# A second network's first layer as seven half products instead of eight (Strassen's scheme, one level), in a fused attention and two-network kernel

## The chip, the core and the metric

The kernel runs on one core of a Trainium2 chip. The metric is device time in microseconds (us) of one execution; the median of 3 runs of the kernel before is 708.27 us (708.18 to 709.79). About 0.3% is what a comparison of this kernel can tell from no change. Engines: PE is TensorE (matmuls; PEld its weight loads), DVE is VectorE, ACT is ScalarE, POOL is GpSimd, SP starts the transfers (DMA).

## What is computed

The reference, cut to what matters here. An attention with random features gives x with 1152 tokens and 512 columns; two networks follow:

```python
def _moe_ref(x, w_in, w_out):            # x 1152 x 512, inner width 2048
    h = x @ w_in
    return (h - np.tanh(h)) @ w_out

def _moe2_ref(x, domain_probs, w1, w2):  # E = 4 experts, inner width F = 1024
    p = domain_probs / (domain_probs.sum(-1, keepdims=True) + 1e-09)
    out = np.zeros((N, D))
    for e in range(E):
        h = np.maximum(x @ w1[e], 0.0)
        out += p[:, e:e + 1] * (h @ w2[e])
    return out
```

The change is in `x @ w1[e]` of the second network.

## The kernel before

Every float32 operand of a product is held as a high and a low part (`split`, L70 and L71: ACT writes the high part, DVE or POOL the rest), and a product is three matmuls: high by high, high by low, low by high. Sums run in PSUM, which has 8 banks of 512 float32 columns.

The kernel has three stages. Attention lies first; while it ends, `early` computes the first network's first layer for its first unit, in the PSUM tiles `ps_e` (2 banks). The pools of attention are opened in the order `ps_e`, `ps_t`, `ps_p`, `ps_n`, two banks each, and closed together. The first network then runs in 4 units of 512 inner columns: `hidden` (L433) computes 128 inner columns for all 1152 tokens in three blocks of 384, `minus_tanh` the activation (L443 to L452, with L450 as the last reader of the PSUM tile), `out_a` (L536) the second layer. Its orders on PE, DVE and ACT are written by hand (`tc.manual_schedule`).

The second network runs in 8 units of 512 inner columns, two for each expert, of 4 steps with 128 each. A step is `hidden` (36 matmuls of 384 columns: 4 parts of the contraction, 3 splits, 3 token blocks), `activated` (ACT L463 writes the high part of the ReLU, DVE L464 the low part), and a quarter of the previous unit's output: `out_b(i, t)` for token tile t is 12 matmuls of 512 columns into a tile of `ps_o` (2 banks, L558), and DVE adds that, times the expert's share, to `oacc` (L562; L560 in the first unit). The order is the planner's: a list of instructions by priority of program order, with buffers that make one wait for another. The weights come by DMA (four of 256 KB for two steps) into `rawp` (4 buffers) and are split by ACT and DVE.

Where things lie: the activations g of a unit are in pool `hpa` for even units and in `hpb` for odd ones; the second layer's weights in `wp` for even and in `wp2` for odd units. After attention the PSUM pools are opened in the order `ps_hb` (3 banks), `ps_ha` (3 banks), `ps_o` (2 banks). The `x` operands of the second network are `x2` (named y in the trace).

Of the kernel before, what the change touches and what calls it, by code (L numbers as in the profile page):

```python
# [18 lines left out]
T2 = 0.01  # L19
# [7 lines left out]
def tile_favor_attention__then__two_moe(  # L27
# [18 lines left out]
    nc = tc.nc  # L46
    B, H, S, D = q.shape
    M = omega.shape[0]
    N, DM = out.shape
# [8 lines left out]
    NJ = UF // P  # L58
    CH = 384
    NC = N // CH  # L60
    scale = 1.0 / float(D) ** 0.25
    assert B == 2 and 2 * D == P and M == P and S == TB * P + P // 2 and NT == 2 * TB + 1

# [5 lines left out]
    def split(hi, lo, src, eng_lo=None):  # L69
        nc.scalar.activation(hi, src, AF.Copy)  # L70
        (eng_lo or nc.vector).tensor_tensor(out=lo, in0=src, in1=hi.bitcast(F32), op=ALU.subtract)  # L71

    def run(todo):
        for step in todo:
            step()

    def interleave(*streams):

        todo = []
        for i, s in enumerate(streams):  # L80
# [4 lines left out]
    units = [("a", u) for u in range(DFF // UF)] + [("b", e, f) for e in range(E) for f in range(F // UF)]  # L85
    NA = DFF // UF
    steps = [(i, j) for i in range(len(units)) for j in range(NJ)]
    wa, wb, late = {}, {}, {}

    class Decoded:  # L90
# [14 lines left out]
        def topped(self):  # L105


            m = self.m = decp.tile([P, UF], I32, tag="m", name="m", bufs=3)
            nc.scalar.activation(m, self.low.bitcast(U32), AF.Copy, scale=2.0**-29 * (1 - 2.0**-18), bias=-0.49999)  # L109

        def joined(self):
            if self.m is None:
                m = self.m = decp.tile([P, UF], I32, tag="m", name="m", bufs=3)
# [31 lines left out]

    def load_a(i, j):

        f0 = units[i][-1] * UF + j * P
        if units[i][0] == "a":
            return Decoded(w_in[:, f0:f0 + P].rearrange("(c p) n -> p c n", p=P), "wa")  # L150
        return Loaded(w1[units[i][1], :, f0:f0 + P].rearrange("(c p) n -> p c n", p=P), "wa", wp)

    def load_b(i, j):

        f0 = units[i][-1] * UF
        if units[i][0] == "a":
            return Decoded(w_out[f0:f0 + UF, j * P:(j + 1) * P].rearrange("(c p) n -> p c n", p=P), "wb")
        rows = w2[units[i][1], f0 + j * P:f0 + (j + 1) * P, :]
        return Loaded(rows.rearrange("p (c n) -> p c n", c=1), "wb", late["wp"] if i % 2 else wp)
# [295 lines left out]
    def activated(i, j, eng_lo=None):  # L455
        new_g(i, j)
        hh, hl = gs[i, j]
        ps = ph[i, j][:, :, :CH]
        if units[i][0] == "a":
# [84 lines left out]
    def out_b(i, t):  # L544

        e = units[i][1]
        if i == NA and t == 0:
            state["acc"] = accp.tile([P, NT, DM], F32, tag="acc", name="oacc")
        s = slice(t * P, (t + 1) * P)
        last = (i, t) == (len(units) - 1, NT - 1)  # L550
        for c in (slice(0, DM // 2), slice(DM // 2, DM)) if last else (slice(0, DM),):
            acc = state["acc"][:, t, c]
            full = ps_o.tile([P, 512], F32, tag="o", name="po")
            po = full[:, :c.stop - c.start]
            for j in range(NJ):
                (wh, wl), (gh, gl) = wb[i, j], gs[i, j]
                for z, (w, g) in enumerate(((wh, gh), (wl, gh), (wh, gl))):
                    nc.tensor.matmul(po, g[:, s], w[:, c], start=j == 0 and z == 0, stop=j == NJ - 1 and z == 2)  # L558
            if i == NA:
# [5 lines left out]
            if i == len(units) - 1:  # L565
                for b in range(B):
                    for t0, t1, r0, r1, ss in token_rows(b):
                        if t0 <= t < t1:
                            rows = out[b * S + ss.start:b * S + ss.stop, c].rearrange("(r t) c -> r t c", t=t1 - t0)
                            nc.sync.dma_start(out=rows[:, t - t0, :], in_=acc[r0:r1, :])  # L570

    def out_steps(i, j):
        return [lambda t=t: out_b(i, t) for t in range(j * NT // NJ, (j + 1) * NT // NJ)]

# [23 lines left out]
    with tc.manual_schedule(engines={mybir.EngineType.DVE, mybir.EngineType.PE, mybir.EngineType.Activation}):  # L598
# [40 lines left out]
    for s in range(END, END + 3):  # L639
        ready(load_a, wa, *steps[s])  # L640
    moe1.close()
    late["wp"] = ctx.enter_context(tc.tile_pool(name="wp2", bufs=NJ, side="right", reuse_waits="tile"))
# [10 lines left out]
    for n in range(1, NC):  # L653
        for j in range(2):
            hidden(NA, j, [n])
    for s in range(NA * NJ, len(steps) + NJ):
        i, j = steps[s] if s < len(steps) else (len(units), s - len(steps))
        g = []
        if s < len(steps):
            if s - NA * NJ > 1:  # L660
                hidden(i, j)
            g = activated(i, j)
            ready(load_b, wb, i, j)
            if s + 3 < len(steps):
                ready(load_a, wa, *steps[s + 3])
        interleave(g, out_steps(i - 1, j) if i > NA else [])


# [28 lines left out]
```

## Time and profile before

| | before |
|---|---|
| median of 3 runs | 708.27 us (708.18 to 709.79) |
| the profiled execution, its own time | 710.09 us |
| its span, first to last instruction | 708.2 us |
| PE busy | 691.7 us (98%) |
| DVE busy | 387.3 us (55%) |
| ACT busy | 287.8 us (41%) |
| mean granted clock of PE | 0.998 |

Attention ends at about 110 us, the first network at about 310, and the second takes the rest. Matmuls overlap, so the busy time of PE counts stretches in which at least one runs; the price of one in a dense stream is the distance from its start to the next one's.

### The profile page before, as it was taken

How to read it: one execution, taken by the hardware profiler on the slowest of the kernel's cores; microseconds unless marked ns; L12 is line 12 of the kernel's file. 1: busy time of each engine (PE TensorE's matmuls, PEld its weight loads, DVE VectorE, ACT ScalarE, POOL GpSimd, SP SyncE). 2: the span in 40 equal slices, each digit the busy share in tenths (PEclk: the TensorE clock that was granted, in tenths of full speed). 3: DMA queues.
4: the chain of work that ended last, by engine and by line, in shares of the span. 5: the costliest groups of instructions: out<-in, count | busy, mean ns of one | idle time of the engine just before them, and what ended most of it. 6: DMA issues, size and time to landing. Idle time of an engine off the chain costs nothing.

```text
span 708.2 us, 9667 instructions
## 1 busy us (share of the span) xinstructions
PE 691.7 (98%) x3897; PEld 643.8 (91%) x3897; DVE 387.3 (55%) x562; ACT 287.8 (41%) x517; POOL 60.3 (9%) x58
## 2 busy tenths in 40 slices
PE   6999998999999999999999999999999999999998
PEld 6999897999999999899898998989989899998986
DVE  4699888699999887554325234234332333243132
ACT  5799897777576674243113012112122121030100
POOL 1032024322221210000000000000000000000000
PEclk9999999999999999999999999999999999999999
DMA  8952100122122110032103012012102111000012
GB/s 218 288 169 90 62 31 5 57 86 94 60 90 90 59 61 31 1 89 90 31 16 88 17 30 75 16 31 75 31 24 66 30 60 46 15 16 1 0 45 89
DMA packets 50412, 43.69 MB, mean 62 GB/s; under 512 B 6080, under 2 KB 45248, under 8 KB 50368
## 3 DMA queue, kind: packets, MB, share of 16 engines
q1 hardware_dynamic: 50368, 43.09, 20.2%
q8 instruction: 30, 0.49, 0.3%
q14 instruction: 14, 0.11, 0.1%
HBM read 40.72 MB, written 2.36 MB: 61 GB/s over the span
## 4 chain that ended last, share of the span: by engine, by line
PE 78%; DVE 11%; ACT 6%; issue 2%; DMA 2%; SPq 1%; POOL 0%; DVEq 0%
PE psh L433 32%; PE po L558 28%; PE po L536 7%; PE pse L433 3%; PE psP L292 3%; PE psN L344 2%; DVE y L450 2%; DVE y L447 2%; DVE y L448 1%; ACT y L444 1%; DVE psh L449 1%; DVE m L119 1%; ACT u L443 1%; DVE m L118 1%; ACT m L109 1%
## 5 line engine op out<-in xcount | busy, mean ns | idle before, releaser
L433 PE MATMUL psh<-y,wah 128*128 128x384 f32 x768 | 157.2, 336 | 0.1
L433 PEld LDWEIGHTS psh<-y,wah 128*128 128x128 f32 x768 | 135.7, 188 | 3.5 <-issue 0.4
L558 PE MATMUL po<-wbl,hh 128*128 128x512 f32 (+1 forms) x292 | 114.4, 392 | 0.0
L558 PE MATMUL po<-wbh,hh 128*128 128x512 f32 (+1 forms) x292 | 113.9, 390 | 0.0
L558 PE MATMUL po<-wbh,hl 128*128 128x512 f32 (+1 forms) x292 | 113.3, 389 | 0.0
L70 ACT ACTIVATE wah<-raw 128x512 fp32r<-128x512 f32 x32 | 20.2, 633 | 201.6 <-PE psh L433 201.6
L433 PE MATMUL psh<-y,wal 128*128 128x384 f32 x384 | 89.9, 336 | 0.0
L562 DVE SCALAR_TENSOR_TENSOR oacc<-po,pr,oacc 128x512 f32<-128x512 f32 (+1 forms) x64 | 47.5, 742 | 74.1 <-PE po L558 74.1
L71 DVE TENSOR_TENSOR wal<-raw,wah 128x512 fp32r<-128x512 f32 x32 | 22.1, 691 | 118.4 <-ACT wah L70 118.3
L433 PEld LDWEIGHTS psh<-y,wal 128*128 128x128 f32 x384 | 68.6, 188 | 0.0
L558 PEld LDWEIGHTS po<-wbh,hl 128*128 128x128 f32 x292 | 54.9, 188 | 12.2
L558 PEld LDWEIGHTS po<-wbh,hh 128*128 128x128 f32 x292 | 54.8, 188 | 11.4
L558 PEld LDWEIGHTS po<-wbl,hh 128*128 128x128 f32 x292 | 54.9, 188 | 10.7
L464 DVE SCALAR_TENSOR_TENSOR hl<-psh,hh 128x1152 fp32r<-128x1152 f32 x32 | 43.4, 1357 | 34.5 <-ACT hh L463 34.4
L536 PE MATMUL po<-hh,wbh 128*128 128x384 f32 x180 | 60.9, 339 | 0.2
L536 PE MATMUL po<-hl,wbh 128*128 128x384 f32 x180 | 60.8, 338 | 0.2
L536 PE MATMUL po<-hh,wbl 128*128 128x384 f32 x180 | 60.6, 336 | 0.5 <-POOL wbl L71 0.5
L433 PE MATMUL psh<-x,wah 128*128 128x384 f32 x288 | 57.9, 336 | 0.6 <-ACT wah L70 0.6
L433 PEld LDWEIGHTS psh<-x,wah 128*128 128x128 f32 x288 | 50.5, 188 | 0.8 <-ACT wah L70 0.8
L463 ACT ACTIVATE hh<-psh 128x1152 fp32r<-128x1152 f32 x32 | 35.8, 1120 | 37.7 <-PE psh L433 37.7
L70 ACT ACTIVATE wbh<-raw 128x512 fp32r<-128x512 f32 x32 | 20.3, 633 | 63.4 <-PE po L558 30.6
L451 ACT ACTIVATE hh<-y 128x1152 fp32r<-128x1152 f32 (+3 forms) x24 | 20.4, 848 | 42.9 <-DVE y L450 42.9
(102 smaller groups left out, 1050.1 us busy)
## 6 DMA issues: line engine op xcount, KB each, us to landing
raw<-in_moe_w_dram SPq DMA_DIRECT2D x64, 256.0 KB, 2.7
raw<-in_moe_w_in_dram SPq DMA_DIRECT2D x16, 512.0 KB, 3.7
raw<-in_moe_w_out_dram SPq DMA_DIRECT2D x16, 512.0 KB, 3.4
kn<-in_k_dram SPq DMA_DIRECT2D x8, 256.0 KB, 4.1
vs<-in_v_dram SPq DMA_DIRECT2D x8, 256.0 KB, 4.6
qn<-in_q_dram SPq DMA_DIRECT2D x8, 256.0 KB, 4.9
out_dram<-oacc SPq DMA_DIRECT2D x7, 256.0 KB, 2.3
out_dram<-oacc SPq DMA_DIRECT2D x4, 128.0 KB, 2.1
```

The lines of the kernel that those rows point to most:

```text
L70: nc.scalar.activation(hi, src, AF.Copy)
L71: (eng_lo or nc.vector).tensor_tensor(out=lo, in0=src, in1=hi.bitcast(F32), op=ALU.subtract)
L292: nc.tensor.matmul(ps[:, i].rearrange("p a m -> p (a m)"), x[:, c], o, start=j == 0, stop=j == 2)
L344: nc.tensor.matmul(ps[:, j, h, :ZC], qt[g][:, j, h, :], kvz[p][:, t // (TB + 1), h, :], start=True, stop=True)
L433: nc.tensor.matmul(ph[i, j][:, n, :CH] if bank is None else bank, w[:, c], x[:, n * CH:(n + 1) * CH] if bank is None else x[:, n], start=z ...
L447: a=lambda: vec.scalar_tensor_tensor(out=y, in0=y, scalar=CB, in1=u, op0=ALU.add, op1=ALU.mult),
L451: h=lambda: act.activation(hh, y, AF.Copy),
L463: lambda: nc.scalar.activation(grid(hh), ps, AF.Relu),
L464: lambda: nc.vector.scalar_tensor_tensor(out=grid(hl), in0=ps, scalar=0.0, in1=grid(hh).bitcast(F32), op0=ALU.max, op1=ALU.subtract),
L536: nc.tensor.matmul(po[:, :CH], w[:, r], g[:, s], start=j == 0 and z == 0, stop=j == NJ - 1 and z == 2,)
L558: nc.tensor.matmul(po, g[:, s], w[:, c], start=j == 0 and z == 0, stop=j == NJ - 1 and z == 2)
L562: nc.vector.scalar_tensor_tensor(out=acc, in0=po, scalar=pr[:, t, e:e + 1], in1=acc, op0=ALU.mult, op1=ALU.add)
```

## The change

The second network's inner columns are cut into 16 pairs (`pairs`) of 2 x 128. For the last 14 of them (`PLAIN = 2` pairs stay as they were) the product of a pair's weights (a 2 x 2 matrix of blocks: 2 halves of inner columns, 2 halves of the contraction) with x (2 halves of the contraction, 2 halves of 576 tokens) is made by Strassen's scheme in Winograd's form: seven products of blocks in place of eight, each 2 contraction parts x 3 splits x 2 column blocks of 288. Sums of x (`token_sums`, T1 to T4) are made once, by DVE, and split; sums of weights (`Sums.added`, S1 to S4) are made by DVE for each pair and split, one pair ahead. Three PSUM tiles of two banks (`ps_y`: Y1, Y2, Y3) take the products, some accumulate on what stands there, and DVE adds across them (`add`). ACT then writes the high and DVE the low part of the ReLU, quarter by quarter.

A unit is now a pair, so an output block `O(t)` has 6 matmuls and DVE adds 144 times to `oacc` in place of 72. `O(t)` of the pair before stands between the products; `o[t]` is its addition on DVE. The order on PE, DVE and ACT is by hand from the third pair on. g of the second network is always in `hpb`, the second layer's weights always in `wp`. `hpa` holds the token sums. `ps_o` is opened ahead of `ps_hb` and `ps_ha`, and these two are closed before `ps_y` is opened. The tiles `m` grow from 512 to 576 elements.

```diff
+    pairs = [(e, f) for e in range(E) for f in range(0, F, 2 * P)]
+    PLAIN = 2
...
-        pool = late["hpb"] if i % 2 else hpa
+        pool = late["hpb"] if i % 2 or i >= NA else hpa
...
+    ps_o = ctx.enter_context(tc.tile_pool(name="ps_o", bufs=2, space=bass.MemoryType.PSUM, reuse_waits="tile"))
+    plain = ExitStack()
     for z in ("ps_hb", "ps_ha"):
-        late[z] = ctx.enter_context(tc.tile_pool(name=z, bufs=1, space=bass.MemoryType.PSUM, reuse_waits="tile"))
-    ps_o = ctx.enter_context(tc.tile_pool(name="ps_o", bufs=2, space=bass.MemoryType.PSUM, reuse_waits="tile"))
+        late[z] = plain.enter_context(tc.tile_pool(name=z, bufs=1, space=bass.MemoryType.PSUM, reuse_waits="tile"))
...
+    def token_sums():
...
+        for name, tag, x, y in (("T1", "y", B12, B11), ("T2", "y", B22, "T1"), ("T4", "t", B21, "T2"), ("T3", "u", B22, B12)):
+            T[name] = gp.tile([P, N], F32, tag=tag, name=tag, bufs=1 + (tag == "y")).rearrange("p (k n) -> p k n", k=2)
+            nc.vector.tensor_tensor(out=T[name], in0=x, in1=T.get(y, y) if isinstance(y, str) else y, op=ALU.subtract)
+        for name in ("T2", "T1", "T3", "T4"):
+            hi, lo = (hpa.tile([P, N], F32R, tag="h" + z, name="T" + z).rearrange("p (k n) -> p k n", k=2) for z in "hl")
+            split(hi, lo, T[name])
...
+    def product(lhs, name, x, ps, first):
+
+        wh, wl = lhs[name]
+        for kk in range(2):
+            xh, xl = rhs[x][kk]
+            for z, (w, b) in enumerate(((wh, xh), (wh, xl), (wl, xh))):
+                for m in range(2):
+                    nc.tensor.matmul(
+                        ps[:, m, :HN // 2], w[:, kk], b[:, m * HN // 2:(m + 1) * HN // 2],
+                        start=first and kk == 0 and z == 0, stop=kk == 1 and z == 2, skip_group_check=not first,
+                    )
...
+    for q in range(1, PLAIN):
+        sums[q + 2] = Sums(q + 2)
+        seconds[q + 1] = Second(q + 1)
+        todo = []
+        for f in range(2):
+            todo.append(lambda f=f: hidden(NA + q, f))
+            todo.append(lambda f=f: run(activated(NA + q, f)))
+        outs = [lambda t=t: out_b(q - 1, t)() for t in range(NT)]
+        interleave(todo[:2] + second(q)[:2] + todo[2:] + second(q)[2:], outs, weights(q + 1))
+    plain.close()
+    ps_y = ctx.enter_context(tc.tile_pool(name="ps_y", bufs=1, space=bass.MemoryType.PSUM, reuse_waits="tile"))
...
+            product(lhs, "A11", "B11", Y1, True)
+            nc.scalar.activation(p1, y1, AF.Copy)
+            run(W[:1])
+            O(0)
+            product(lhs, "S2", "T2", Y2, True)
+            run(W[1:2])
+            o[0]()
+            add(y2, p1, u2)
+            run(W[2:3])
+            O(1)
+            product(lhs, "A12", "B21", Y1, False)
+            run(W[3:5])
+            o[1]()
+            O(2)
+            high(y1, 0, 0)
+            run(W[5:7])
+            product(lhs, "S1", "T1", Y2, False)
+            low(y1, 0, 0)
+            o[2]()
+            O(3)
+            run(W[7:])
+            add(y2, p1, u4)
+            product(lhs, "S3", "T3", Y3, True)
+            o[3]()
+            O(4)
+            run(W2[:1])
+            add(y3, u4, u4)
+            product(lhs, "S4", "B22", Y2, False)
+            high(u4, 1, 1)
+            run(W2[1:2])
+            o[4]()
+            O(5)
+            low(u4, 1, 1)
+            add(y2, p1, y2)
+            product(lhs, "A22", "T4", Y3, False)
+            high(y2, 0, 1)
+            o[5]()
+            O(6)
+            low(y2, 0, 1)
+            add(y3, u2, y3)
+            O(7)
+            high(y3, 1, 0)
+            run(W2[2:3])
+            o[6]()
+            low(y3, 1, 0)
+            O(8)
+            o[7]()
+            run(W2[3:])
+            o[8]()
```

`W` are the eight steps that make the next pair's weights (`added`, `high` on ACT, `low` on DVE), `W2` the four that split the pair's second-layer weights.

## Rows read from the trace of the kernel before

**Rows 1.** The page: busy time of PE, and its granted clock in 40 slices.

```profile
PE 691.7 (98%) x3897; PEld 643.8 (91%) x3897; DVE 387.3 (55%) x562; ACT 287.8 (41%) x517; POOL 60.3 (9%) x58
PEclk9999999999999999999999999999999999999999
```

**Rows 2.** Chain of waits, second network: start us, us, engine, tile, line, instructions.

```profile
318.37 18.96 PE psh L433 x108
...
480.15 6.24 PE psh L433 x36
486.39 5.49 PE po L558 x24
```

**Rows 3.** Stretches, busy us of PE, PEld, DVE, ACT, POOL; clock; DMA.

```profile
125.00:284.00 159.00, 157.13 (x900) 155.18 (x899) 136.83 (x148) 108.23 (x136) 34.02 (x25) 1.00 0.22 68
...
430.00:530.00 100.00, 100.00 (x506) 90.69 (x506) 35.43 (x44) 18.32 (x24) 0.00 (x0) 1.00 0.14 43
```

**Rows 4.** Single matmuls of L558 in order of time: start us, listed duration.

```profile
348.07 0.39 PE L558 MATMUL po<-wbh,hh 128*128 128x512 f32 x1
...
350.87 0.40 PE L558 MATMUL po<-wbh,hh 128*128 128x512 f32 x1
...
386.39 0.39 PE L558 MATMUL po<-wbh,hh 128*128 128x512 f32 x1
...
389.37 0.39 PE L558 MATMUL po<-wbl,hh 128*128 128x512 f32 x1
...
701.77 0.28 PE L558 MATMUL po<-wbl,hh 128*128 128x256 f32 x1
...
704.37 0.28 PE L558 MATMUL po<-wbh,hl 128*128 128x256 f32 x1
```

**Rows 5.** Groups by line and shape: count, busy us, mean ns, idle before, releaser.

```profile
L562 DVE SCALAR_TENSOR_TENSOR oacc<-po,pr,oacc 128x512 f32<-128x512 f32 x62 | 46.5, 751 | 72.5 <-PE po L558 72.5
L464 DVE SCALAR_TENSOR_TENSOR hl<-psh,hh 128x1152 fp32r<-128x1152 f32 x32 | 43.4, 1357 | 34.5 <-ACT hh L463 34.4
L463 ACT ACTIVATE hh<-psh 128x1152 fp32r<-128x1152 f32 x32 | 35.8, 1120 | 37.7 <-PE psh L433 37.7
L71 DVE TENSOR_TENSOR wal<-raw,wah 128x512 fp32r<-128x512 f32 x32 | 22.1, 691 | 118.4 <-ACT wah L70 118.3
L70 ACT ACTIVATE wah<-raw 128x512 fp32r<-128x512 f32 x32 | 20.2, 633 | 201.6 <-PE psh L433 201.6
L449 DVE TENSOR_TENSOR pse<-pse,t 128x256 f32<-128x256 f32 x4 | 1.7, 426 | 0.0
```

**Rows 6.** PE and DVE in order of time where attention meets the first network.

```profile
124.17 0.34 PE L536 MATMUL po<-hh,wbh 128*128 128x384 f32 x1
...
126.63 0.34 PE L536 MATMUL po<-hl,wbh 128*128 128x384 f32 x1
...
127.78 0.46 DVE L450 COPY_PREDICATED y<-u,pse 128x256 f32<-128x256 int32 x1 [0.35 <-ACT u L446]
...
130.25 0.46 DVE L450 COPY_PREDICATED y<-u,pse 128x256 f32<-128x256 int32 x1
```

**Rows 7.** PE in order of time after two gaps; idle time and releaser in brackets.

```profile
112.74 0.62 PE L433 MATMUL pse<-x,wah 128*128 128x384 f32 x2 [1.46 <-DVE y L450]
...
284.02 0.45 PE L536 MATMUL psh<-hh,wbh 128*128 128x384 f32 x1 [0.90 <-ACT hh L451]
```

**Rows 8.** Stretches around the same two gaps, columns as in rows 3.

```profile
284.00:288.50 4.50, 3.53 (x11) 3.27 (x12) 1.48 (x2) 0.00 (x0) 0.00 (x0) 0.65 0.00 0
...
110.90:117.50 6.60, 4.41 (x27) 3.65 (x25) 4.63 (x10) 5.31 (x12) 2.03 (x2) 1.00 0.00 0
```

**Rows 9.** DVE's last split between the networks, and a handoff from ACT to DVE.

```profile
310.26 0.56 DVE L71 TENSOR_TENSOR y<-acc,y 128x384 fp32r<-128x384 f32 x1
...
486.45 1.12 ACT L463 ACTIVATE hh<-psh 128x1152 fp32r<-128x1152 f32 x1
...
487.60 1.36 DVE L464 SCALAR_TENSOR_TENSOR hl<-psh,hh 128x1152 fp32r<-128x1152 f32 x1 [0.33 <-ACT hh L463]
```

More of the change, by code (lines that the diff above doesn't have):

```diff
@@ L60, in tile_favor_attention__then__two_moe @@
     NC = N // CH
+    HN = N // 2
     scale = 1.0 / float(D) ** 0.25
@@ L82, in interleave @@
         run(step for _, _, step in sorted(todo, key=lambda z: z[:2]))
-    units = [("a", u) for u in range(DFF // UF)] + [("b", e, f) for e in range(E) for f in range(F // UF)]
+    units = [("a", u) for u in range(DFF // UF)]
     NA = DFF // UF
-    steps = [(i, j) for i in range(len(units)) for j in range(NJ)]
+    steps = [(i, j) for i in range(NA) for j in range(NJ)]
+    pairs = [(e, f) for e in range(E) for f in range(0, F, 2 * P)]
+    PLAIN = 2
     wa, wb, late = {}, {}, {}
@@ L458, in activated @@
         ps = ph[i, j][:, :, :CH]
-        if units[i][0] == "a":
+        if i < NA:
             t, u, y = (late["gp"].tile([P, N], F32, tag=z, name=z, bufs=1 + (z == "y")) for z in "tuy")
@@ L542, in out_a @@
         return lambda: nc.vector.tensor_tensor(out=acc, in0=po[:, :CH], in1=acc, op=ALU.add)
-    def out_b(i, t):
-        e = units[i][1]
-        if i == NA and t == 0:
+    rhs = {}
+    def token_sums():
+        acc, gp = state["acc"], late["gp"]
+        B11, B12, B21, B22 = (acc[:, 2 * k:2 * k + 2, h * HN:(h + 1) * HN] for k in range(2) for h in range(2))
+        T = {}
+        for name, tag, x, y in (("T1", "y", B12, B11), ("T2", "y", B22, "T1"), ("T4", "t", B21, "T2"), ("T3", "u", B22, B12)):
[4 more added lines that the diff above has]
+            split(hi, lo, T[name])
+            rhs[name] = [(hi[:, kk], lo[:, kk]) for kk in range(2)]
+        x2 = state["x"]
+        for name, k, h in (("B11", 0, 0), ("B21", 1, 0), ("B22", 1, 1)):
+            rhs[name] = [tuple(z[:, h * HN:(h + 1) * HN] for z in x2[2 * k + kk]) for kk in range(2)]
@@ new lines, in tile_favor_attention__then__two_moe, with __init__, added, _dest @@
+    class Sums:
+        def __init__(self, q):
+            e, f = pairs[q]
+            self.q = q
+            raw = rawp.tile([P, KD * 2 * P], F32, tag="raw", name="raw")
+            raw = raw.rearrange("p (c n) -> p c n", n=2 * P)
+            nc.sync.dma_start(out=raw, in_=w1[e, :, f:f + 2 * P].rearrange("(c p) n -> p c n", p=P))
+            self.A = [[raw[:, 2 * k:2 * k + 2, g * P:(g + 1) * P] for k in range(2)] for g in range(2)]
+            self.row = raw[:, :, :P]
+            self.lhs = {}
+        def added(self, i):
+            if i == 0:
+                self.S = [decp.tile([P, UF], F32, tag="y", name="y").rearrange("p (s k n) -> p s k n", s=2, n=P) for _ in range(2)]
+            S = [self.S[z // 2][:, z % 2] for z in range(4)]
+            (A11, A12), (A21, A22) = self.A
+            x, y, op = (
+                (A21, A22, ALU.add), (S[0], A11, ALU.subtract), (A11, A21, ALU.subtract), (A12, S[1], ALU.subtract),
+            )[i]
+            nc.vector.tensor_tensor(out=S[i], in0=x, in1=y, op=op)
+        def _dest(self, i):
+            src, names = (
+                (self.row, ("A11", "A12")), (self.S[0], ("S1", "S2")), (self.S[1], ("S3", "S4")), (self.A[1][1], ("A22",)),
+            )[i]
+            return src, names
+        def high(self, i):
+            src, names = self._dest(i)
+            pool = wp if self.q % 2 else late["wp"]
+            w = [pool.tile([P, UF], F32R, tag="wa" + z, name="wa" + z) for z in "hl"]
+            w = [x.rearrange("p (s k n) -> p s k n", s=2, n=P) for x in w]
+            for s, name in enumerate(names):
+                self.lhs[name] = (w[0][:, s], w[1][:, s])
+            if i == 0:
+                w = [x.rearrange("p s k n -> p (s k) n") for x in w]
+            elif i == 3:
+                w = [x[:, 0] for x in w]
+            self.w = src, w[0], w[1]
+            nc.scalar.activation(w[0], src, AF.Copy)
+        def low(self):
+            src, hi, lo = self.w
+            nc.vector.tensor_tensor(out=lo, in0=src, in1=hi.bitcast(F32), op=ALU.subtract)
@@ new lines, in tile_favor_attention__then__two_moe, with __init__, high, low @@
+    class Second:
+        def __init__(self, q):
+            e, f = pairs[q]
+            self.q = q
+            self.raw = rawp.tile([P, 2 * DM], F32, tag="raw", name="raw").rearrange("p (j n) -> p j n", j=2)
+            nc.sync.dma_start(out=self.raw, in_=w2[e, f:f + 2 * P, :].rearrange("(j p) n -> p j n", p=P))
+        def high(self, j):
+            wb[NA + self.q, j] = tuple(wp.tile([P, UF], F32R, tag="wb" + z, name="wb" + z) for z in "hl")
+            nc.scalar.activation(wb[NA + self.q, j][0], self.raw[:, j], AF.Copy)
+        def low(self, j):
+            hi, lo = wb[NA + self.q, j]
+            nc.vector.tensor_tensor(out=lo, in0=self.raw[:, j], in1=hi.bitcast(F32), op=ALU.subtract)
@@ L548, in out_b, with add @@
+    def out_b(q, t, cols=slice(0, DM)):
+        i = NA + q
+        e = pairs[q][0]
+        if q == 0 and t == 0:
             state["acc"] = accp.tile([P, NT, DM], F32, tag="acc", name="oacc")
         s = slice(t * P, (t + 1) * P)
[L550 to L559, printed above, removed]
+        acc = state["acc"][:, t, cols]
+        po = ps_o.tile([P, 512], F32, tag="o", name="po")[:, :cols.stop - cols.start]
+        for j in range(2):
+            (wh, wl), (gh, gl) = wb[i, j], gs[i, j]
+            for z, (w, g) in enumerate(((wh, gh), (wl, gh), (wh, gl))):
+                nc.tensor.matmul(po, g[:, s], w[:, cols], start=j == 0 and z == 0, stop=j == 1 and z == 2)
+        def add():
+            if q == 0:
@@ L564, in out_b @@
                 )
-            if i == len(units) - 1:
+            if q == len(pairs) - 1:
                 for b in range(B):
@@ L568, in out_b @@
                         if t0 <= t < t1:
-                            rows = out[b * S + ss.start:b * S + ss.stop, c].rearrange("(r t) c -> r t c", t=t1 - t0)
+                            rows = out[b * S + ss.start:b * S + ss.stop, cols].rearrange("(r t) c -> r t c", t=t1 - t0)
                             nc.sync.dma_start(out=rows[:, t - t0, :], in_=acc[r0:r1, :])
-    def out_steps(i, j):
-        return [lambda t=t: out_b(i, t) for t in range(j * NT // NJ, (j + 1) * NT // NJ)]
+        return add
     END = NA * NJ
@@ L638, in tile_favor_attention__then__two_moe @@
         ends = {(c, n): out_a(NA - 1, c, n, [NJ - 1]) for c, n in last[:5]}
[L639 to L642, printed above, removed]
+    for f in range(2):
+        ready(load_a, wa, NA, f)
     x2 = [[xp.tile([P, N], F32R, tag=f"x{a}{c}", name=f"y{a}{c}") for a in range(2)] for c in range(KD)]
@@ L655, in tile_favor_attention__then__two_moe @@
             hidden(NA, j, [n])
[L656 to L666, printed above, removed]
+    for f in range(2):
+        run(activated(NA, f))
+        ready(load_a, wa, NA + 1, f)
@@ new lines, in tile_favor_attention__then__two_moe, with weights @@
+    seconds = {0: Second(0), 1: Second(1)}
+    for j in range(2):
+        seconds[0].high(j)
+        seconds[0].low(j)
+    token_sums()
+    moe1.close()
+    late["wp"] = ctx.enter_context(tc.tile_pool(name="wp2", bufs=NJ, side="right", reuse_waits="tile"))
+    sums = {PLAIN: Sums(PLAIN)}
+    def weights(q):
+        x = sums.get(q)
+        if x is None:
+            return []
+        return [
+            lambda: (x.added(0), x.high(0)), lambda: (x.low(), x.added(1)), lambda: (x.high(1), x.added(2)),
+            lambda: (x.low(), x.added(3)), lambda: x.high(2), lambda: x.low(), lambda: x.high(3), lambda: x.low(),
+        ]
@@ new lines, in second @@
+    def second(q):
+        x = seconds[q]
+        return [lambda: x.high(0), lambda: x.low(0), lambda: x.high(1), lambda: x.low(1)]
+    for q in range(1, PLAIN):
+        sums[q + 2] = Sums(q + 2)
+        seconds[q + 1] = Second(q + 1)
+        todo = []
+        for f in range(2):
+            todo.append(lambda f=f: hidden(NA + q, f))
+            todo.append(lambda f=f: run(activated(NA + q, f)))
+        outs = [lambda t=t: out_b(q - 1, t)() for t in range(NT)]
+        interleave(todo[:2] + second(q)[:2] + todo[2:] + second(q)[2:], outs, weights(q + 1))
@@ new lines, in tile_favor_attention__then__two_moe, with halves, O, add @@
+    plain.close()
+    ps_y = ctx.enter_context(tc.tile_pool(name="ps_y", bufs=1, space=bass.MemoryType.PSUM, reuse_waits="tile"))
+    MN = HN // 2
+    def halves(t):
+        return t.rearrange("p (m n) -> p m n", m=2)
+    with tc.manual_schedule(engines={mybir.EngineType.DVE, mybir.EngineType.PE, mybir.EngineType.Activation}):
+        for q in range(PLAIN, len(pairs)):
+            if q + 2 < len(pairs):
+                sums[q + 2] = Sums(q + 2)
+            if q + 1 < len(pairs):
+                seconds[q + 1] = Second(q + 1)
+            W, W2 = weights(q + 1), second(q)
+            lhs = sums[q].lhs
+            for f in range(2):
+                new_g(NA + q, f)
+            Y1, Y2, Y3 = (ps_y.tile([P, 2, 512], F32, tag=f"Y{z}", name=f"Y{z}") for z in (1, 2, 3))
+            y1, y2, y3 = (y[:, :, :MN] for y in (Y1, Y2, Y3))
+            p1, u2, u4 = (halves(decp.tile([P, HN], F32, tag="m", name=z, bufs=3)) for z in ("p1", "u2", "u4"))
+            o = {}
+            def O(t):
+                o[t] = out_b(q - 1, t)
+            def add(x, y, to):
+                nc.vector.tensor_tensor(out=to, in0=x, in1=y, op=ALU.add)
+            def high(x, f, h):
+                nc.scalar.activation(halves(gs[NA + q, f][0][:, h * HN:(h + 1) * HN]), x, AF.Relu)
+            def low(x, f, h):
+                gh, gl = (halves(z[:, h * HN:(h + 1) * HN]) for z in gs[NA + q, f])
+                nc.vector.scalar_tensor_tensor(out=gl, in0=x, scalar=0.0, in1=gh.bitcast(F32), op0=ALU.max, op1=ALU.subtract)
+            product(lhs, "A11", "B11", Y1, True)
[47 more added lines that the diff above has]
+            o[8]()
@@ L670 @@
+    for t in range(NT):
+        for c in (slice(0, DM // 2), slice(DM // 2, DM)) if t == NT - 1 else (slice(0, DM),):
+            out_b(len(pairs) - 1, t, c)()
 _INS = ['q', 'k', 'v', 'omega', 'moe_w_in', 'moe_w_out', 'moe2_domain_probs', 'moe2_w1', 'moe2_w2']
```

16 lines of the change are left out of this document (7 added, 9 removed).

## The prediction

> **What bounds the kernel now.** I read the page's busy times first, then the chain of waits, then stretches and single instructions on the chain. TensorE (PE) is busy 98% of the span at a granted clock of 0.9 or more of full speed in every slice [rows 1], and in the second network the chain is nothing but its matmuls: blocks of first-layer products (L433) and output products (L558) follow each other with no other engine between [rows 2]. In 100 us of that part PE has no idle time, VectorE (DVE) is busy 35 us, ScalarE (ACT) 18 [rows 3]. So this part costs what PE's matmuls cost, and the spare time of DVE is what the change can spend.
>
> The price of a matmul is the distance between starts, not its listed duration (0.39 us at 512 columns), since matmuls overlap. From first and last row of a dense stretch: 256 columns (704.37-701.77)/22 = 118.2 ns [rows 4]; 384 columns 6.24/36 = 173.4 ns [rows 2]; 512 columns 229.2 ns (13 steps) in one kind of unit and 233.3 ns (12 steps) in the other [rows 4]; the chain has the first again as 5.49/24 [rows 2]. 256, 384 and the cheaper 512 lie on one line: 0.43 ns a column plus 7.6 ns. On it 288 columns cost 118.2 + 32 x 0.431 = 132.0 ns.
>
> **First layer.** The second network is 16 pairs of 256 inner columns. A pair now takes 2 x 36 matmuls of 384 columns: 72 x 173.4 ns = 12.49 us. A pair in the new scheme takes 7 products x 2 x 3 x 2 = 84 matmuls of 288 columns: 84 x 132.0 ns = 11.09 us. So 1/8 fewer columns, but 12 more matmuls with their fixed part: 1.40 us a pair, and 14 of 16 pairs: **-19.6 us**. The scheme breaks even where a 288-column matmul costs 12.49/84 = 148.6 ns. Bounds for its price: 130.0 (in proportion to 384) and 136, if these operands draw the 4 ns that one kind of 512-column block draws; that is -2.4 and +4.7 us over 1,176 matmuls. I take the line.
>
> Beside these rows stands a rule that speaks against the change: the Trainium skill, "TensorE: Matmul & The Clock Gate", section "Back-to-back issue gap", gives a sustained stream of weight loads and matmuls 81 ns each at 128 columns and 131 ns at 512. On the straight line between them, as an estimate from that page, 288 columns would cost 102 ns and 384 114 ns, so a pair 8.57 against 8.23 us and the change would lose 4.7 us. The trace disagrees: 229 ns at 512.
>
> **Output products.** The same 864 matmuls of 512 columns, as 16 x 9 blocks of 6 in place of 8 x 9 of 12. What moves is where their operands lie. Dear blocks (233 ns) have g in hpa and weights in wp, cheap ones (229) g in hpb and weights in wp2; after the change g is always in hpb, the weights always in wp. Neither kind shows that mix: 432 x 4.1 ns = +-1.8 us; I take 0, both being equally near.
>
> **DVE and ACT in a pair.** No PE time by itself, if covered. DVE by rows [rows 5]: nine accumulations into oacc instead of 4.5, 9 x 0.75 = 6.8; four sums of weights at 256 elements, 4 x 0.43 = 1.7; low parts of weights 5 x 0.69 + 0.43 = 3.9; four sums of products and four low parts at 576 elements, between the rows for 256 (0.43) and 1152 (1.36) 0.76 each, 6.1. Sum 18.4 us, where PE needs 11.09 + 54 x 0.231 = 23.6. It is now about 3.4 + 2.8 + 2.7 = 9 a half unit. ACT: highs 5 x 0.63 + 0.4, five tiles of 576 at 0.65, 6.8. So both fit; whether in order too I get by laying the hand-written orders on one line (PE blocks 1.58 and 1.40 us, 0.2 for the drain: listed duration less spacing). The nearest places: block O(8) starts at 22.3 and waits for accumulation o[6], queued behind the last sum on Y3, done at 21.8; S4 starts at 14.9, its Y2 is read out (u4) by 11.5; A22 at 17.9, Y3 read by 14.5; the next pair's O(0) at 25.3, its g (the last low part) ready at 22.6. Behind DVE's wait for the weights' first high part (1.4 to 3.1) queue o[0] and u2; both end 2.6 us or more before PE wants the space. The smallest slack is 0.45 us, and that wait ends on PE's own O(6). I charge 0 a pair. With the cover gone, each late step costs PE its lateness, up to the 1.4 us of a block.
>
> **Move of the PSUM pools.** ps_o is now opened ahead of ps_hb and ps_ha, because ps_y takes their place later. Pools are stacked in order, so I read it that ps_o gets the banks of ps_e (opened first in attention), that it had the last ones before, and that the big tiles move behind it. Then the first output block of the first network needs the bank that the last-but-one early activation releases. Now that block starts at 124.17 with four matmuls and ends 8 matmuls after 126.63 [rows 6]. The L450 that reads the bank last ends at 127.78 + 0.46 = 128.24 [rows 6], so all 12 matmuls (2.08) come after: end 130.3 instead of 128.0. Queued behind it on PE, in the hand order, is the whole rest of the first network, where PE is busy 157.1 of 159 us [rows 3], so nothing absorbs it: **+2.3 us**. The second block's bank (130.25 + 0.46 [rows 6]) is just free by then. Bounds: 0 if the banks fall otherwise, and +3.9 if the clock follows. At 284 PE had stood idle for 0.90 us [rows 7], and the 4.5 us from there show a mean granted clock of 0.65 [rows 8], so most of them went at the 1.2 GHz level: 4.5 x 0.35 = 1.6 us lost. Yet a gap of 1.46 us before 112.74 [rows 7] left it at 1.00 [rows 8]. I take no drop.
>
> **Between the networks.** token_sums adds to DVE four differences and four low parts of 1152 elements, 8 x 1.36 = 10.9 us, behind the splits that end at 310.8 [rows 9], with 5.5 us of lows ahead: until about 327. The accumulations of pair 0 queue behind it. PE meanwhile has the first layer of pairs 0 and 1 (the block of 108 matmuls, 19 us, starts at 318.4 now [rows 2]; 72 of them remain), and two output blocks into ps_o: dense until 333, if the planner fills so; then DVE has some 15 us of work for PE's nine blocks, which is close: **+0.5 us**, bounds 0 and +3.2 (two stalls of a block, if output blocks are put ahead of pair 1's layer). The loads, two of 512 KB a pair in place of four of 256, are issued a whole pair before their use: hidden. Tail and last halves stay.
>
> **Sum.** -19.6 + 0 + 2.3 + 0.5 = -16.8. The profiled run's own time is 710.09 (span 708.2 and 1.9 around it), which gives 693.3; the median of the runs, 708.27, lies 1.8 lower, and on its scale I forecast **691.5 us**.
>
> **Rivals.** (1) The banks cost nothing: 689.2. For it: the place of a pool is my reading of the order alone. (2) The gap at 126 brings the clock down: 693.1. (3) PE waits in every pair: the orders are tight in three places; with 0.5 to 1.2 us in each of 14 pairs 698 to 708. Against: every wait but one has 1.9 us or more. (4) DVE becomes the bound, and the kernel slower: 27 instructions a pair, most of them behind a wait for another engine. If such a wait costs 0.19 us beyond its row, DVE's 18.4 reach 23.6, and it decides from there; at 0.3 a pair takes 26.5 instead of 24.97, 14 x 1.53 = +21 and the 2.8 of the shifts: 732. Against: L464 starts at 487.60, 0.03 us after the ACT instruction that it waits for (486.45 + 1.12 [rows 9]). (5) A 288-column matmul costs as much as one of 384, its time being set per instruction: 84 x 173.4 ns = 14.57, 14 x 2.08 = +29 and 2.8, 740. Against: 256 columns at 118 ns. Beside it stands the page's rule above, which is milder: by it 4.7 us would be lost and 2.8 in the shifts, 716. (6) That the products are not made: the counts exclude it.
>
> **How the numbers follow.** Forecast 0.55, (1) 0.22, (2) 0.10, (3) 0.07, (4) 0.04, (5) with the page's rule 0.02. The range: down to 686.5 (no bank cost, output at 229 ns, line a little lower), up to 698.5 (288 columns at 136 ns, clock drop, or the mild half of stalls together). A measurement tells 0.3%, 2.1 us, from no change: faster 0.92, same 0.02 (the end of (3)), slower 0.06.
>
> **What would show it.** Starts of the products 132 ns apart and twelve in 1.58 us; output blocks at 229 to 233 ns; PE idle in a pair near 0, DVE busy 18 of 23.6 us; PE waiting for L450 before the first output block near 126 to 128, and the first network's end 2.3 us later. It is wrong if products start more than 140 ns apart, if PE waits for DVE in each pair, or if the granted clock falls in the second network.

## The result, and the profile after

| | before | after |
|---|---|---|
| median | 709.03 us (708.18 to 710.06, 4 runs) | 691.91 us (690.38 to 694.46, 4 runs) |
| ratio, 95% interval | | 0.9762 (0.9727 to 0.9796) |
| the profiled execution, own time and span | 710.09, 708.2 | 694.46, 692.6 |
| PE, DVE, ACT busy | 691.7, 387.3, 287.8 | 671.7, 530.7, 318.0 |

The kernel is 17.1 us faster (14.5 to 19.4 by the interval) where 16.8 were forecast. Before's median has moved from 708.27 to 709.03 with a fourth run. The page after, against [rows 1]:

```profile
PE 671.7 (97%) x4059; PEld 624.7 (90%) x4059; DVE 530.7 (77%) x824; ACT 318.0 (46%) x591; POOL 61.3 (9%) x58
PEclk9999999999999999999999999999999999999999
```

162 more matmuls, 20 us less of PE, 143 us more of DVE. The chain of waits in one pair of each kind (start us, us, instructions), which answers to [rows 2]; L643 are the products, L660 the output blocks:

```profile
418.60 1.59 PE Y L643 x12
420.19 1.40 PE po L660 x6
421.59 1.59 PE Y L643 x12
...
438.04 4.13 PE po L660 x18
442.16 1.57 PE Y L643 x12
...
461.34 4.08 PE po L660 x18
```

A product takes 1.57 or 1.59 us, so a matmul of 288 columns about 131 or 132.5 ns (131.2 and 132.5 from start to start). The two kinds of pair differ in the place of their first-layer weights (wp2 or wp). Stretches of one pair each and of 13 pairs, columns as in [rows 3]:

```profile
395.35:418.60 23.25, 23.25 (x140) 21.15 (x140) 17.83 (x29) 6.42 (x11) 0.00 (x0) 1.00 0.17 46
418.60:442.16 23.56, 23.56 (x141) 21.27 (x140) 17.91 (x29) 6.43 (x11) 0.00 (x0) 1.00 0.16 45
...
350.00:660.00 310.00, 310.00 (x1831) 281.04 (x1830) 234.22 (x366) 84.20 (x144) 0.00 (x0) 1.00 0.14 40
```

A pair takes 23.4 us on average, and PE has no idle time in 310 us: none of the waits laid out in the prediction reaches it. Where attention meets the first network, PE and DVE in order of time, against [rows 6]:

```profile
125.79 0.51 PE L435 MATMUL pse<-x,wah 128*128 128x256 f32 x2 [0.85 <-DVE y L452]
...
129.28 0.44 PE L539 MATMUL po<-hh,wbh 128*128 128x384 f32 x1 [1.81 <-DVE y L452]
...
130.36 0.53 PE L539 MATMUL po<-hh,wbl 128*128 128x384 f32 x1
...
132.28 0.53 PE L539 MATMUL po<-hh,wbl 128*128 128x384 f32 x1
...
128.78 0.44 DVE L452 COPY_PREDICATED y<-u,pse 128x256 f32<-128x256 int32 x1
```

PE stands idle for 1.81 us until L452 (before's L450) has read its PSUM tile (128.78 + 0.44 = 129.22), and the block starts at 129.28. From its sixth matmul on the distance is 0.32 us in place of 0.17: the clock is at its 1.2 GHz level, for 11 matmuls or 3.4 us. Once that is over, PE is 5.0 us later than in the trace of before; ahead of the block it was 0.6 later. So 4.4 us are lost here.

### The profile page after: what moved, and what is told of

The parts are those of the page before. It is cut to its first block, busy times and chain, and to the rows that moved or that the text cites. A ratio compares the mean times of both kernels' runs of the same rounds, so it can differ in the third digit from the quotient of the medians.

```text
span 692.6 us, 10155 instructions
## 1 busy us (share of the span) xinstructions
PE 671.7 (97%) x4059; PEld 624.7 (90%) x4059; DVE 530.7 (77%) x824; ACT 318.0 (46%) x591; POOL 61.3 (9%) x58
## 4 chain that ended last, share of the span: by engine, by line
PE 75%; DVE 13%; ACT 6%; issue 2%; DMA 1%; SPq 1%; POOL 0%; DVEq 0%; POOLq 0%
PE po L660 28%; PE Y L643 22%; PE psh L435 7%; PE po L539 6%; PE pse L435 3%; PE psP L294 2%; PE psN L346 2%; DVE y L449 2%; DVE y L452 2%; DVE y L450 1%; ACT y L446 1%; DVE psh L451 1%; ACT u L445 1%; DVE m L123 1%; DVE m L122 1%
## 5 line engine op out<-in xcount | busy, mean ns | idle before, releaser
L666 DVE SCALAR_TENSOR_TENSOR oacc<-po,pr,oacc 128x512 f32<-128x512 f32 (+1 forms) x136 | 101.4, 746 | 34.2 <-PE po L660 33.8
L660 PE MATMUL po<-wbh,hl 128*128 128x512 f32 x290 | 112.9, 389 | 0.4 <-DVE hl L466 0.4
L660 PE MATMUL po<-wbh,hh 128*128 128x512 f32 x290 | 112.9, 389 | 0.1
L660 PE MATMUL po<-wbl,hh 128*128 128x512 f32 x290 | 112.9, 389 | 0.0
L660 PEld LDWEIGHTS po<-wbh,hl 128*128 128x128 f32 x290 | 54.4, 188 | 12.3 <-DVE hl L466 0.8
L660 PEld LDWEIGHTS po<-wbh,hh 128*128 128x128 f32 x290 | 54.7, 188 | 8.2 <-DVE oacc L666 0.3
L660 PEld LDWEIGHTS po<-wbl,hh 128*128 128x128 f32 x290 | 54.4, 188 | 7.5
L643 PE MATMUL Y<-y,wah 128*128 128x288 f32 x336 | 57.9, 294 | 0.0
L643 PEld LDWEIGHTS Y<-y,wah 128*128 128x128 f32 x336 | 51.2, 188 | 3.6 <-DVE hl L466 0.3
L643 PE MATMUL Y<-Th,wal 128*128 128x288 f32 x224 | 47.8, 295 | 0.0
L643 PE MATMUL Y<-Tl,wah 128*128 128x288 f32 x224 | 47.6, 294 | 0.0
L643 PE MATMUL Y<-Th,wah 128*128 128x288 f32 x224 | 47.6, 293 | 0.0
L643 PEld LDWEIGHTS Y<-Th,wah 128*128 128x128 f32 x224 | 39.0, 188 | 4.5
```

What stands on the lines that cost most here:

```text
L643: nc.tensor.matmul(ps[:, m, :HN // 2], w[:, kk], b[:, m * HN // 2:(m + 1) * HN // 2], start=first and kk == 0 and z == 0, stop=kk == 1 and ...
L660: nc.tensor.matmul(po, g[:, s], w[:, cols], start=j == 0 and z == 0, stop=j == 1 and z == 2)
L666: nc.vector.scalar_tensor_tensor(out=acc, in0=po, scalar=pr[:, t, e:e + 1], in1=acc, op0=ALU.mult, op1=ALU.add)
```

## The experiments

Each kernel was timed beside runs of before on the same chip (medians 709.35 to 709.61). "Changed kernel" is the one after, 691.91, which was timed beside before at 709.03.

**e1_banks: the changed kernel with other banks.**

```diff
-    ps_e = actx.enter_context(tc.tile_pool(name="ps_e", ...))
...
     ps_n = actx.enter_context(tc.tile_pool(name="ps_n", ...))
+    ps_e = actx.enter_context(tc.tile_pool(name="ps_e", ...))
...
-    for z in ("ps_hb", "ps_ha"):
+    for z in ("ps_ha", "ps_hb"):
```

> The changed kernel with other PSUM banks: attention opens ps_e last instead of first, and ps_ha is opened ahead of ps_hb, so that the output tiles ps_o lie on banks that attention left at about 111 us (those of ps_t) and the early activations' banks 6 and 7 go to ps_hb, which is first written some 14 us later. Nothing else is changed. Theory (the first output block of the first network waits for the bank that an early activation still reads): PE's idle time of 1.81 us ahead of that block is gone, it starts at about 124 and four matmuls of it stand in the gap before the last early block, the clock doesn't fall there, and the time is 2.3 us below the changed kernel where the clock stayed up, up to 4.4 below where it fell: 687.5 to 689.5. Rival (the wait is one for the data of the first output block, or the activation's place in the queues): the gap stays and the time is that of the changed kernel, 690.4 to 694.5.

Measured 688.69 us (687.61 to 690.09, 5 runs), ratio to before 0.9704 (0.9689 to 0.972): 3.2 us below the changed kernel. PE in order of time:

```profile
126.06 0.34 PE L539 MATMUL po<-hh,wbh 128*128 128x384 f32 x1
...
126.58 0.34 PE L539 MATMUL po<-hh,wbh 128*128 128x384 f32 x1
...
128.57 0.34 PE L539 MATMUL po<-hl,wbh 128*128 128x384 f32 x1
```

Four matmuls of the first output block stand again ahead of the last early block, as in [rows 6], and eight behind it; the gap is gone. The stretch around it, columns as in [rows 3]:

```profile
124.00:136.00 12.00, 11.88 (x76) 11.47 (x75) 7.34 (x17) 9.56 (x23) 7.23 (x7) 1.00 0.14 44
```

PE is busy 11.88 of 12 us at a clock of 1.00, where the changed kernel has:

```profile
124.00:136.00 12.00, 9.34 (x50) 8.94 (x50) 6.00 (x13) 7.77 (x18) 5.72 (x7) 0.86 0.14 44
```

So the bank is the cause, and this version beats both kernels: it is 20.7 us below the runs of before beside it, where the changed kernel was 17.1 below.

**e2_pool_alone: the kernel before with the pool order alone.**

```diff
+    ps_o = ctx.enter_context(tc.tile_pool(name="ps_o", bufs=2, ...))
     for z in ("ps_hb", "ps_ha"):
         late[z] = ctx.enter_context(tc.tile_pool(name=z, bufs=1, ...))
-    ps_o = ctx.enter_context(tc.tile_pool(name="ps_o", bufs=2, ...))
```

> The kernel before with one edit of the change alone: ps_o is opened ahead of ps_hb and ps_ha. Theory (the bank): the same gap of about 1.8 us appears before the first output block near 128, the block ends 2.3 us later, and the kernel takes 710.5 to 713.5 (the upper end with the clock down behind the gap) against 709.0. Rival (the later first network of the changed kernel comes from another part of the change, such as the wider tiles m or the planner's other order): no difference from before, within 0.5 us.

Measured 713.46 us (711.63 to 714.9, 6 runs), ratio 1.0058 (1.0041 to 1.0075), 4.1 us slower than before. The gap is there with nothing else of the change (PE in order of time):

```profile
129.05 0.50 PE L536 MATMUL po<-hh,wbh 128*128 128x384 f32 x1 [1.83 <-DVE y L450]
129.35 0.53 PE L536 MATMUL po<-hl,wbh 128*128 128x384 f32 x1
```

In this profiled execution the clock is down from the block's first matmuls on (0.32 us a step from 129.35 on), and the gap costs 4.4 us in all. By medians it costs 4.1, about the forecast's 2.3 and what the clock takes; how many of the six executions had the drop isn't known.

**e3_eight: eight products in place of seven.** The sums of x, of weights and of products are gone with it.

```diff
-            product(lhs, "A11", "B11", Y1, True)
...
+            for n, (f, h) in enumerate(((0, 0), (0, 1), (1, 0), (1, 1))):
+                Y = ps_y.tile([P, 2, 512], F32, tag=f"Y{turn}", name=f"Y{turn}")
+                product(lhs, (f, 0), f"B1{h + 1}", Y, True)
+                O(2 * n)
...
+                product(lhs, (f, 1), f"B2{h + 1}", Y, False)
+                O(2 * n + 1)
```

> The changed kernel with eight half products in place of seven for the 14 pairs: every quarter of a pair's first layer is two products of 12 matmuls of 288 columns that accumulate in PSUM, without sums of x, of weights or of products. Units of 256 columns, orders by hand, output blocks between the products, pool order and places stay. Theory (the gain is the eighth product, the rest of the edit is worth nothing or costs): 14 x 12 x 131.7 ns = 22 us above the changed kernel, 713 to 716, so 4 to 6 slower than before (2.6 for 96 matmuls of 288 columns against 72 of 384, 2.3 or more for the bank). Rival (smaller units and hand orders have a share of the gain): below 710.

Measured 713.19 us (712.82 to 714.25, 6 runs), ratio 1.0058 (1.0045 to 1.0072): 21.3 above the changed kernel, 22 expected. With eight products nothing is gained: the rest of the change, taken together, costs 3.8 us against before. (Its output blocks are as cheap as the changed kernel's, 226 to 233 ns a matmul, so a gain of some 2 us there is inside these 3.8.) Its first output block shows the same gap, this time with the clock up (0.17 us a step), and there it costs 2.8 us:

```profile
128.57 0.45 PE L539 MATMUL po<-hh,wbh 128*128 128x384 f32 x1 [1.83 <-DVE y L452]
...
130.58 0.34 PE L539 MATMUL po<-hh,wbl 128*128 128x384 f32 x1
```

**e4_aligned: operands at other starts.**

```diff
+    padl = const.tile([P, 24], F32, name="padl")
+    padr = padp.tile([P, 120], F32, name="padr")
```

> The changed kernel with two unused tiles (96 bytes on the left, 480 on the right of SBUF), which move the weights wp and the operands x2, T and wp2 from starts 416 and 480 bytes behind a multiple of 512 to multiples of 512; g follows to 256 behind one. Theory A (the start of an operand within a line of memory sets the few ns by which matmuls of the same width differ: products 131.0 in pairs of weights in wp2, 132.5 with weights in wp; output blocks 227 and 230 ns): the dear pairs fall to the cheap ones' 23.25 us or below, 7 x 0.3 = 2 us or more gained, 688 to 690. Theory B (the difference comes from somewhere else, such as which weights lie far from the moving operand): pairs of 23.25 and 23.56 us alternate as now and the time stays.

Measured 691.98 us (691.74 to 695.93, 5 runs), ratio 0.9767 (0.9745 to 0.9788). The chain of waits:

```profile
411.48 4.10 PE po L665 x18
415.59 1.58 PE Y L648 x12
417.17 1.38 PE po L665 x6
...
434.97 4.10 PE po L665 x18
```

The two kinds of pair are one now, 23.49 us long (411.48 to 434.97), which is 0.1 above the mean of the two before. Weights in wp still lie on the left and those in wp2 on the right, so distance (theory B's example) doesn't make the difference: moving the starts does change these few ns, as theory A has it, but nothing is gained by multiples of 512, and its forecast fails. Which operand's start it is stays open. The pairs are what to compare here, not the whole times: in this trace attention ends in another order, and a gap of 1.79 us stands ahead of the last early block (125.94) and none ahead of the first output block.

**e5_dve4, e6_dve9, e9_dve14: more work for DVE.** The added instructions write an unused tile, at four places of a pair (e5), at nine (e6), and fourteen in all with a second one at every other place (e9). The diff is that of e5.

```diff
+            def more(t):
+                if t in (1, 3, 5, 7):
+                    nc.vector.tensor_tensor(out=junk, in0=junk, in1=junk, op=ALU.max)
...
             o[1]()
+            more(1)
```

> The changed kernel with four more DVE instructions in each of the 14 pairs (one pass of 512 elements over an unused tile behind the additions o[1], o[3], o[5], o[7]; 0.69 us each by its kind, 2.8 us a pair). Nothing waits for them but DVE's own queue. Theory (DVE has 5.5 us of spare time in a pair of 23.4, and the orders have enough slack): DVE busy 20.6 us a pair, PE without idle time, the time that of the changed kernel, 690.5 to 694.5. Rival (the orders are tight, each late step costs PE its lateness): pairs of 24 us or more, 700 or above.

> As the run with four more DVE instructions, with nine in each pair, one behind every addition: 6.2 us. Theory (the bound turns to DVE once its work passes PE's 23.4 us): DVE's 17.9 + 6.2 = 24.1 us a pair and, ahead of the low part of the weights, a wait of up to 1.75 us for ACT that can't all be filled; so pairs of 24.1 to 25.9 us, PE idle 0.7 to 2.5 us in each, 10 to 35 us longer: 702 to 727. Rival (DVE's work is not what bounds, since its instructions overlap at their ends by some 0.07 us): no change, below 695.

Measured 693.06 us (691.24 to 693.57, 4 runs) with four and 692.17 (691.51 to 692.72, 4 runs) with nine: no difference from the changed kernel's 691.91. The forecast for nine failed. Stretches with nine:

```profile
350.00:660.00 310.00, 310.00 (x1831) 281.06 (x1830) 296.10 (x486) 82.07 (x143) 0.00 (x0) 1.00 0.13 40
```

PE has no idle time while DVE is busy 296 of 310 us (busy time counts a stretch that two instructions share once). DVE in order of time says why the load is lower than the forecast had it:

```profile
401.47 0.74 DVE L668 SCALAR_TENSOR_TENSOR oacc<-po,pr,oacc 128x512 f32<-128x512 f32 x1
402.13 0.68 DVE L821 TENSOR_TENSOR junk<-junk 128x512 f32<-128x512 f32 x1
402.73 0.42 DVE L619 TENSOR_TENSOR wal<-raw,wah 128x256 fp32r<-128x256 f32 x1
403.06 0.75 DVE L824 TENSOR_TENSOR u<-Y,p 128x576 f32<-128x576 f32 x1
```

An instruction listed with 0.74 us is followed after 0.66, one with 0.68 after 0.60, one with 0.42 after 0.33. In a full queue the load is the sum of these distances, about 0.08 us an instruction less than the sum of durations. The third run was to show where it ends:

> As the runs with four and nine more DVE instructions, with fourteen in each pair (two behind o[0], o[2], o[4], o[6] and o[8], one behind the others), to find where DVE begins to bound. In the run with nine the starts of DVE instructions in a row stand closer than their durations: 0.60 us for 0.68, 0.66 for 0.75, 0.33 for 0.42. Theory (DVE's load is the sum of the distances between starts: about 16.0 us a pair in the changed kernel, 21.4 with nine more, where PE still had no idle time): 16.0 + 14 x 0.60 = 24.4 us against PE's 23.4, with what waits are left up to 25.5, so 1.0 to 2.1 us a pair: 705 to 722. Rival A (the sum of durations, 17.9 + 14 x 0.68 = 27.4, beyond some point): 748. Rival B (no bound here either): below 695.

Measured 721.28 us (720.51 to 721.61, 4 runs), at the theory's upper end: 29.4 above the changed kernel. A pair takes 25.65 us from start to start. Stretches, PE in order of time, and PE's waits from 360 to 660 (us in all, times, longest):

```profile
360.00:660.00 300.00, 284.74 (x1620) 245.73 (x1619) 297.95 (x492) 73.69 (x128) 0.00 (x0) 1.00 0.13 40
```

```profile
444.62 0.50 PE L662 MATMUL po<-wbh,hh 128*128 128x512 f32 x1 [0.95 <-DVE oacc L668]
```

```profile
PE po L662 <- DVE oacc L668: 14.3, 23, 0.9
```

Now DVE is full (0.17 us of a pair idle) and PE waits for it, for room in ps_o above all. So the 25.65 us are DVE's own load, and not 24.4 and waits, as the expectation had it. Two things were left out of its 24.4. A pair has 28 instructions of DVE and not 27: `add` stands five times in the listing, not four. And a second added instruction, which reads what the one ahead of it has just written, starts 0.03 us after that one's end in place of 0.08 before it.

**e7_cols144: half the width.** Four matmuls of 144 columns in place of two of 288.

```diff
-                for m in range(2):
+                for m in range(4):
...
-                        ps[:, m, :HN // 2], w[:, kk], b[:, m * HN // 2:(m + 1) * HN // 2],
+                        ps[:, m // 2, m % 2 * HN // 4:(m % 2 + 1) * HN // 4], w[:, kk], b[:, m * HN // 4:(m + 1) * HN // 4],
```

> The changed kernel with each product's matmuls cut to 144 columns: 24 in place of 12 for a product, the same columns in all, four blocks on two PSUM banks. It measures what a matmul of half the width costs in the stream. Theory A (the line of the rows of before, 7.6 ns and 0.431 ns a column, goes on): 69.7 ns each, a pair 168 x 69.7 = 11.7 us of products in place of 11.06, 9 us more: 699 to 703. Theory B (below some width the loading of 128 x 128 weights, which each matmul has, sets the distance): a price that no longer falls with the columns, between 69.7 and 118.2 ns (the row for 256), so up to 19.9 us a pair, 124 us more.

Measured 803.1 us (1 run). The chain of waits:

```profile
411.17 2.63 PE Y L643 x24
413.81 1.43 PE po L660 x6
```

2.63/24 = 109.8 ns a matmul, not 69.7: the price is theory B's. Pairs take 31.1 us, 7.7 more than in the changed kernel, 7.4 of them in the products. By groups, the weight loads of these products keep their duration:

```profile
L643 PEld LDWEIGHTS Y<-y,wah 128*128 128x128 f32 x672 | 84.9, 191 | 3.6 <-DVE hl L466 0.3
```

Twice as many matmuls of half the columns pay 110 ns each, little less than the 118 of 256 columns. If 110 ns is a floor that holds from there up, which one width doesn't show, it meets the line of the wider ones at (109.8 - 7.6)/0.431 = 237 columns, an estimate. Beside this result stands the Trainium skill, "TensorE: Matmul & The Clock Gate", section "LDWEIGHTS (loading the stationary operand)", by whose formula 128 columns of weights take 107 ns, an estimate from that page: the trace agrees within 3%, as a distance in a stream, while the listed duration is 191. That it is the load of the weights that sets the 110 ns, and not another cost of each matmul, is argued and not shown: no run changes the loads alone.

**e10_planner: no orders by hand in the second network.**

```diff
-    with tc.manual_schedule(engines={mybir.EngineType.DVE, mybir.EngineType.PE, mybir.EngineType.Activation}):
+    with ExitStack():
         for q in range(PLAIN, len(pairs)):
```

> The changed kernel without the orders by hand in the second network: the same instructions in the same program order, but the planner orders PE, DVE and ACT by its own costs from the third pair on. Theory (the gain lies in the columns saved, and any order that keeps PE fed gives it, since DVE and ACT have spare time): the time of the changed kernel, 690 to 695. Rival (the order by hand is what covers the handoffs): PE idle in each pair, 1 us or more of it, 705 or above.

Measured 693.03 us (690.1 to 693.71, 4 runs), ratio 0.9776 (0.976 to 0.9793). Stretches:

```profile
350.00:660.00 310.00, 310.00 (x1831) 281.03 (x1831) 228.56 (x356) 86.39 (x140) 0.00 (x0) 1.00 0.11 36
```

PE has no idle time in the planner's order either. With the program order as it stands, which the planner follows as its priority, the orders by hand are worth nothing that can be measured here.

## Why the prediction was right, point by point

**First layer, -19.6.** Right. 288 columns cost 131.2 and 132.5 ns, mean 131.9, where the line gave 132.0; a pair's products 11.08 us. 14 x (12.49 - 11.08) = 19.7. That the rest of the change, taken together, brings no gain is shown by e3_eight.

**Output products, 0 with bounds of 1.8.** A pair's 54 matmuls take 23.4 - 11.08 = 12.3 us, 228.3 ns each against 231.2 on average before. For 14 pairs that is 2.2 us less, so the term lay a little beyond its lower bound: the mix of places that no row showed is on average as cheap as the cheap one (226.5 ns in one kind of pair, 230.1 in the other). e4_aligned shows that operands' starts matter to such differences, but not which.

**DVE and ACT, no PE time.** Right in the result, but the size of DVE's load was off twice, and the errors partly cancel. The prediction counts four sums of products where the listing has five (L818 starts at 399.89, 405.76, 408.69, 411.63 and 414.56 in the pair from 395.35 on), so the durations add up to 19.1 us and not 18.4. And it takes durations for the load: in a full queue each of the 28 instructions costs 0.08 us less, which leaves about 16.8. The 17.9 us busy lie between the two because the queue is full only in part. So the room was larger than forecast: nine more instructions fit, and fourteen make DVE the bound. Rival (4), by which DVE would pay more than its rows, fell: in these pairs it pays less. That the reads of Y2 and Y3 end well ahead of PE, as laid out, agrees with PE's idle time of zero; that the order by hand is needed for it was not claimed, and e10_planner shows that it isn't.

**Move of the pools, +2.3.** Right in mechanism, shown by e1_banks and e2_pool_alone from both sides: 3.2 us gained by taking it away, 4.1 lost by adding it alone. So rival (1) is out. The wait itself ends with L452, as forecast. The profiled execution shows rival (2) as well: the clock falls behind the gap, 11 matmuls at 0.32 us, some 1.6 us. In e3_eight the same gap left the clock up. By the starts of the second output block's first matmul in the two traces, less what was lost ahead of it, the gap's whole price is 2.4 us (e6_dve9, e9_dve14, e10_planner) or 2.8 (e3_eight) with the clock up, and 4.4 with it down (the changed kernel, e2_pool_alone, e5_dve4, e7_cols144). So the forecast of no drop holds for some executions and not for others; among the four of the changed kernel the slowest has a mean granted clock of 0.995 and the fastest 1.000. The row that the prediction set beside it, the clock's fall at 284, doesn't stand behind one gap either: 0.95 us more are idle ahead of 285.42, and the clock falls only then.

**Between the networks, +0.5.** Right. From the first product of the second network to the first of the scheme's, in the kernel after:

```profile
294.86:348.70 53.84, 53.43 (x287) 49.98 (x287) 37.13 (x51) 18.82 (x27) 0.00 (x0) 1.00 0.09 30
```

PE idles 0.4 us, with DVE busy 37: token_sums costs next to nothing. Its last instruction ends at 327.8 (forecast 327). The 0.4 us are one wait, and not for the accumulations, as forecast, but for the low part of the first pair's activations, which stands in DVE's queue behind part of the token sums:

```profile
322.67 1.35 DVE L466 SCALAR_TENSOR_TENSOR hl<-psh,hh 128x1152 fp32r<-128x1152 f32 x1
...
324.07 0.49 PE L660 MATMUL po<-wbh,hl 128*128 128x512 f32 x1 [0.39 <-DVE hl L466]
```

**The sum.** In the profiled executions the spans differ by 15.6: 19.7 and 2.2 gained, 4.4 lost by the gap and the clock behind it, 0.4 between the networks. Two small losses no step has. 0.6 us stand ahead of the first early block behind the gap of 1.46 us (113.37 in place of 112.74, against [rows 7]); this is scatter, since the traces of e5 to e10 reach that block between 0.7 us earlier and 0.7 us later than before does. And 0.3 us stand in a wait for ACT at the end of the first network, 1.20 us in place of 0.90 (0.92 in e3_eight, which makes no sums):

```profile
289.33 0.45 PE L539 MATMUL psh<-hh,wbh 128*128 128x384 f32 x1 [1.20 <-ACT hh L453]
```

The last 0.6 us were not traced to a cause. By medians 16.8 was forecast and 17.1 measured. That these agree within 0.3 us is in part luck: the output products gave 2.2 us that the sum has not, and the move of the pools cost 3.2 to 4.1 by medians in place of 2.3.

**Rivals (3) to (5)** fell: no PE wait in a pair, DVE not full, a price that follows the columns. Rival (5) had more in it than its 0.02 says: at half the width a matmul costs nearly what one of 256 columns does (e7_cols144), and by the estimate above 288 columns lie only 51 above the point where that begins. This stream has 110 ns at 144 columns, 118 at 256 and 229 at 512; the figures that the prediction gave from the Trainium skill, "TensorE: Matmul & The Clock Gate", section "Back-to-back issue gap" (81 ns at 128 columns, 131 at 512), are not those of it.

## What to carry to other kernels

Take a matmul's price from the distance between starts at two or three widths, and check that the new width lies between them: below them the line need not go on. Here a product in matmuls of 144 columns took 2.63 us, where the same columns took 1.58 in matmuls of 288. A change in the order in which PSUM pools are opened moves banks under code that it doesn't touch, and the first writer of a bank then waits for another last reader; here it cost 3 to 4 us and was taken back by moving one pool and swapping two. Count a second engine's load by the distances in a full queue before calling it tight.

## What was not expected of the hardware

Matmuls of 144 columns, each with a weight load listed with 191 ns, start 110 ns apart: the listed duration of a load is not its price in a stream. DVE instructions in a full queue start 0.08 us before the one ahead of them is listed as ended.

The wait ahead of the first output block stands in eight traces, with a shorter one (0.8 us) ahead of the early block before it. PE's clock fell behind it in four of them (0.86 on the mean over 124 to 136 in the changed kernel, e2_pool_alone, e5_dve4 and e7_cols144; waits of 1.81 to 1.83 us) and stayed up in four (1.00 in e3_eight, with 1.83 us, and in e6_dve9, e9_dve14 and e10_planner, with 1.48 or 1.49):

```profile
124.00:136.00 12.00, 9.74 (x61) 9.33 (x61) 6.41 (x16) 7.75 (x18) 5.77 (x6) 1.00 0.13 43
```

This is the stretch in e6_dve9. At the end of the first network every trace, that of before too, has two waits of about a microsecond, and there the clock fell in six of eleven.
